# A leaky unit in one ScalarE instruction, and a shorter split of float64 weights, in an attention + two-layer MLP kernel

## The chip, the cores and the metric

One core of one Trainium2 chip runs the whole program in one launch. The metric is the device time in microseconds (us). A core has five engines that matter here: PE (TensorE, matmuls), DVE (VectorE), ACT (ScalarE), POOL (GpSimd) and SP (SyncE, which issues the DMAs). Each executes its own queue in order, and they meet at semaphores.

## The reference

```python
x = attention(q, k, v, M_prev, z_prev, beta)     # 2304 tokens x 512, causal softmax + a linear memory, gated
h = x @ w_in                                     # 512 -> 2048
x = np.maximum(0.01 * h, h) @ w_out              # the leaky unit; 2048 -> 512
a = x @ w_a                                      # 512 -> 1536
b = x @ w_b
out = (a * b @ w_out2).astype(np.float32)        # 1536 -> 512
```

The weights arrive as float64 and the activations as float32. The kernel carries both through the matmuls as two parts, a high one in the fp32r format and the float32 remainder of it, also kept as fp32r.

## The kernel before, in words

**Three stages.** An attention stage (lines 235 to 763) works on 16 pairs of heads. Its instructions are not written out in order: each step is given to `Plan` with a cost per engine, and `Plan.run` schedules them over 58 forward and backward sweeps and emits the best order found. The costs in the `add(...)` calls decide which engine a step gets and when. Where the plan sees PE idle early on, it inserts filler matmuls (L254). Then `moe1` (L965) and `moe2` (L1014) run in the order in which the Python loops issue them.

**The matmuls.** `three` (L229) issues three matmuls for a product: high x high (L230), high x low (L231), low x high (L232). The tokens are cut in two parts (1024 and 1280 columns), each in chunks `c` of 512 or 256 columns. In `moe1` a group `g` of 256 hidden features is computed for a part in up to six chunks (kind "u": 12 matmuls each into a PSUM bank of the ring `b0, b1, b2, b6`), and then multiplied back (kind "o": 6 matmuls each into the ring `b3, b4, b5, b7`, which L1007 on ACT evacuates in group 0 and L1009 on DVE afterwards). There are 8 groups. `moe2` has 6 groups of the same build with two products per chunk, `a * b` (L1043, DVE) in place of the leaky unit, and evacuations at L1060 (ACT, group 0) and L1062 (DVE).

**The leaky unit** is two instructions for each chunk: L985 on ACT writes 0.01 * h from PSUM to `gf`, and L986 on DVE takes the maximum of h (PSUM) and `gf`. `halves` (L942) then makes the high part on ACT (L944) and the low part on DVE or POOL (L945); it queues them one or two ticks later, so that they stand behind the next chunk's first instructions. The plan holds the first four chunks of group 0 (`first`, L675), with the same two steps at L692 and L696.

**The weights.** `Weights.micro` (L121) turns a chunk `i` of 512 columns of float64, loaded as pairs of 32-bit words, into high and low parts. There are 68 chunks, 4 of them inside the plan. The steps and their engines: `clamp` (L136, DVE) bounds the upper word, read as a float32 at a stride of two words; `square` (L139, ACT) squares it; `shift` (L142, DVE) and `join` (L145, DVE) move the exponent and mantissa to float32's places; `normal` (L148, DVE) multiplies with 0 where the square is too small; `high` (L154, ACT) rounds to fp32r; `power` (L159, DVE) and `low` (L162, DVE) scale the lower word; `rest` (L165) and `total` (L168) form the low part on POOL. `Weights.step` (L186) issues a third of a chunk at a time: clamp and shift (square one tick later), join and normal (high one tick later), power and low (rest and total one tick later). In `moe1` and `moe2` one such third is queued after most of the chunks, up to a limit of tiles held, and `split_parts` (L935) adds the splitting of the activations (L937 ACT, L938 DVE) at the start of each.

Of the kernel before, what the change touches and what calls it, by code (L numbers as in the profile page):

```python
# [11 lines left out]
F32 = mybir.dt.float32  # L12
# [3 lines left out]
AF = mybir.ActivationFunctionType  # L16
ALU = mybir.AluOpType
# [25 lines left out]
TURN = 170.0  # L43
COLD = 1400.0, 7000.0

WMIN = float(np.uint32(897 << 20).view(np.float32))
WMAX = float(np.uint32((1150 << 20) | 0xFFE00).view(np.float32))


# [5 lines left out]
def attention_moe_moe2(ctx: ExitStack, tc, kqT, qn, vn, m_prev, beta, w_in, w_out, w_a, w_b, w_o2, out):  # L55
# [26 lines left out]
    def after(k, fn):  # L82
        now[1] += 1
        heapq.heappush(tasks, (now[0] + k, now[1], fn))
# [7 lines left out]
    class Weights:  # L92
# [28 lines left out]
        def micro(self, i):  # L121

            c = slice((i % 2) * WC, (i % 2) * WC + WC)
            key = f"w{i // 2}.{i % 2}"
            t = {}

            def u(x):
                return t[x].bitcast(U32)

            def half(x):  # L130
                return self.tiles[i // 2][:, x, c]

            def clamp(_):
                for x in "har":
                    t[x] = self.temp(i, [P, WC], F32, "w" + x)
                nc.vector.tensor_scalar(t["h"], self.raw[i][:, :, 1].bitcast(F32), WMAX, -WMAX, ALU.min, ALU.max)  # L136

            def square(_):
                nc.scalar.activation(t["r"], t["h"], AF.Square)  # L139

            def shift(_):
                nc.vector.tensor_scalar(u("a"), u("h"), 3, 0x3FFFFFFF, ALU.logical_shift_left, ALU.bitwise_and)  # L142

            def join(_):
                nc.vector.scalar_tensor_tensor(u("a"), u("h"), 0xC0000000, u("a"), ALU.bitwise_and, ALU.bitwise_or)  # L145

            def normal(_):
                nc.vector.scalar_tensor_tensor(t["a"], t["r"], WMIN * WMIN, t["a"], ALU.is_ge, ALU.mult)  # L148

            def high(eng):  # L150
                if i % 2 == 0:
                    self.tile(i // 2)
                if eng == "ACT":
                    nc.scalar.copy(half(0), t["a"])  # L154
                else:
                    nc.vector.tensor_copy(half(0), t["a"])

            def power(_):
                nc.vector.tensor_scalar(u("h"), u("a"), 0xFF800000, None, ALU.bitwise_and)  # L159

            def low(_):
                nc.vector.scalar_tensor_tensor(t["r"], self.raw.pop(i)[:, :, 0], 2.0**-52, t["h"], ALU.mult, ALU.mult)  # L162

            def rest(eng):
                (nc.gpsimd if eng == "POOL" else nc.vector).tensor_tensor(t["a"], t["a"], f32(half(0)), ALU.subtract)  # L165

            def total(eng):
                (nc.gpsimd if eng == "POOL" else nc.vector).tensor_tensor(half(1), t["a"], t["r"], ALU.add)  # L168

            place = [f"g{x}.0" for x in ("10", "11", "12", "13", "1t")] if i == 2 else []  # L170
            one, two, tt = {"DVE": 335.0}, {"DVE": 600.0}, {"POOL": 1230.0, "DVE": 600.0}
            return [
                (None, lambda _: self.load(i), [], ["wraw"]),
                (one, clamp, ["wraw"], ["wh", "wa", "wr"]),
                ({"ACT": 520.0}, square, ["wh"], ["wr"]),
                (one, shift, ["wh"], ["wa"]),
                (two, join, ["wh"], ["wa"]),
                (two, normal, ["wr"], ["wa"]),
                ({"ACT": 520.0, "DVE": 335.0}, high, ["wa"], [key] + place),
                (one, power, ["wa"], ["wh"]),  # L180
                (two, low, ["wraw", "wh"], ["wr"]),
                (tt, rest, [key], ["wa"]),
                (tt, total, ["wr", "wa"], [key]),
            ]

        def step(self, n=1, limit=RING):  # L186

            for _ in range(n):
                i, third = divmod(self.part, 3)
                if i >= 2 * min(len(self.order), self.freed + limit):  # L190
                    return
                if third == 0:
                    self.load(i)
                    self.load(i + 1)
                    self.steps = [s[1] for s in self.micro(i)]
                _, clamp, square, shift, join, normal, high, power, low, rest, total = self.steps
                if third == 0:
                    clamp(0)
                    after(1, lambda: square(0))
                    shift(0)  # L200
                elif third == 1:
                    join(0)
                    normal(0)
                    after(1, lambda: high("ACT"))
                else:
                    power(0)
                    low(0)
                    after(1, lambda: (rest("POOL"), total("POOL")))
                self.part += 1
# [25 lines left out]
    def attention(att, plan):  # L235
# [22 lines left out]
        def one(key, shape, dtype=F32, pool=att):  # L258
            live[key] = pool.tile(shape, dtype, tag=key, bufs=1, name=key)
            return live[key]  # L260
# [414 lines left out]
        def first(x):  # L675
# [13 lines left out]
            gk = f"gf{x % 3}"  # L689

            def leak(_):
                nc.scalar.activation(one(gk, [P, 512], F32, main), plan.tiles[t], AF.Copy, scale=0.01)  # L692

            def most(_):
                g = live[gk]
                nc.vector.tensor_tensor(g, plan.tiles[t], g, ALU.max)  # L696

            def hi(eng):
                if k == 0:
# [3 lines left out]
            def lo(eng):  # L703
                both(eng, gates[f][:, 1, c], live[gk], f32(gates[f])[:, 0, c], ALU.subtract)

            add(leak, {"ACT": 480}, r=[t], w=[gk], at=at + 6)
            add(most, {"DVE": 600}, r=[t], w=[gk], at=at + 7)
            add(hi, c_copy(512), r=[gk] + [f"{hl}.g0"] * (k > 0), w=[f"{hl}.g{k}"] + ["raw2"] * (k == 0 and f == 1), at=at + 8, port=True)
            add(lo, c_tt(512), r=[gk, f"{hl}.g{k}"], w=[f"{hl}.l{k}"], at=at + 9, port=True)

# [254 lines left out]
    def moe1(ps, xh, y, gates):  # L965
        for g in range(8):
            wi = weights.get().rearrange("p s (k c) -> p s k c", k=4)
            for pr in range(2):
                x = xh[pr]
                gt = gates if g == pr == 0 else []  # L970
                for f in range(0 if gt else 2):
                    t = shared()
                    gt.append(t)
                    for c in chunks(pr):
                        n = c.stop - c.start
                        tick()
                        hp = ring("u", ps, [P, 512], F32)
                        for kt in range(4):
                            w = slice(f * 128, f * 128 + 128)
                            three(  # L980
                                hp[:, 0:n], wi[:, 0, kt, w], wi[:, 1, kt, w], x[:, 0, kt, c], x[:, 1, kt, c],
                                kt == 0, kt == 3,
                            )
                        gf = ring("gf", main, [P, 512], F32)[:, 0:n]
                        nc.scalar.activation(gf, hp[:, 0:n], AF.Copy, scale=0.01)  # L985
                        nc.vector.tensor_tensor(gf, hp[:, 0:n], gf, ALU.max)  # L986
                        halves(t, c, gf, nc.vector if f else nc.gpsimd)
                        yield "u", g, pr
                if pr == 0:
# [192 lines left out]
```

## Time and profile before

| what | value |
|---|---|
| median of 3 runs | 1061.68 us (1060.17 to 1061.82) |
| the profiled execution | 1061.82 us, of which the span of instructions is 1060.0 us |
| PE busy | 1043.9 us (98%) |
| DVE busy | 766.3 us (72%) |
| ACT busy | 426.0 us (40%) |
| POOL busy | 362.0 us (34%) |
| granted TensorE clock | 1.00, the 2.4 GHz level |
| chain that ended last | PE 70%, DVE 25%, ACT 2%, issue 2% |

The profile is one execution. A group of rows gives instructions of one line; its mean mixes those that ran at once and those that stood waiting for a shared resource after they had started. A wait gives the idle time of an engine and what ended it. Matmuls overlap, and their ends are modelled, so the busy share of PE is not a share of its peak.

### The profile page before, as it was taken

The numbers are of one execution on the slowest core, as the hardware profiler recorded it, in microseconds if no ns is written. First come the engines' busy times: TensorE is split into PE (matmuls) and PEld (weight loads), VectorE is DVE, ScalarE is ACT, GpSimd is POOL, SyncE is SP. The second block draws the span as 40 slices with busy tenths as digits, with TensorE's granted clock in tenths as the row PEclk, the third lists the DMA queues.
The fourth block names the chain that finished last, engine by engine and source line by source line (L and its number), as shares of the span: only waits on it lengthen the run. The fifth ranks groups of instructions, "written<-read, shape, count | busy, mean of one in ns | idle before, by whom it ended". The sixth has DMA issues, their size and how long they took to land.

```text
span 1060.0 us, 14629 instructions
## 1 busy us (share of the span) xinstructions
PE 1043.9 (98%) x5432; PEld 828.1 (78%) x5432; DVE 766.3 (72%) x1488; ACT 426.0 (40%) x949; POOL 362.0 (34%) x323
## 2 busy tenths in 40 slices
PE   9999999999999999999999999999999999999998
PEld 4566666787888788888888877888878878878887
DVE  6999999778787878676767693782973964955333
ACT  6888888665333333333333353422222222312110
POOL 4575663235445353342434131330330420411100
PEclk9999999999999999999999999999999999999999
DMA  5333430211111111110111010110110210210022
GB/s 214 102 119 115 159 132 27 73 60 60 40 60 60 40 60 40 40 60 20 60 40 57 3 48 33 60 60 1 61 60 1 80 40 2 80 39 1 1 80 99
DMA packets 18935, 63.33 MB, mean 60 GB/s; under 512 B 2224, under 2 KB 2224, under 8 KB 18864
## 3 DMA queue, kind: packets, MB, share of 16 engines
q1 hardware_dynamic: 18864, 62.40, 16.6%
q8 instruction: 42, 0.69, 0.3%
q14 instruction: 29, 0.24, 0.1%
HBM read 57.68 MB, written 4.72 MB: 59 GB/s over the span
## 4 chain that ended last, share of the span: by engine, by line
PE 70%; DVE 25%; ACT 2%; issue 2%; DMA 0%; DVEq 0%; POOL 0%; ACTq 0%; POOLq 0%
PE b L230 18%; PE b L231 18%; PE b L232 18%; PE b L548 4%; PE b L626 4%; PE b L495 3%; DVE wa L142 3%; DVE wh L136 2%; DVE wa L148 2%; DVE xf L1062 2%; DVE wa L145 2%; DVE wr L162 2%; DVE hl L945 2%; DVE gf L986 1%; PE b L522 1%
## 5 line engine op out<-in xcount | busy, mean ns | idle before, releaser
L230 PE MATMUL b<-xh,w 128*128 128x512 f32 (+1 forms) x800 | 295.5, 369 | 0.0
L231 PE MATMUL b<-xh,w 128*128 128x512 f32 (+1 forms) x800 | 294.6, 368 | 0.0
L232 PE MATMUL b<-xh,w 128*128 128x512 f32 (+1 forms) x800 | 294.4, 368 | 0.0
L165 POOL TENSOR_TENSOR wa<-wa,w 128x512 f32<-128x512 f32 x65 | 112.0, 1722 | 494.1 <-DVE wh L159 430.3
L230 PEld LDWEIGHTS b<-xh,w 128*128 128x128 f32 x800 | 150.8, 189 | 25.4
L232 PEld LDWEIGHTS b<-xh,w 128*128 128x128 f32 x800 | 150.7, 188 | 25.2
L231 PEld LDWEIGHTS b<-xh,w 128*128 128x128 f32 x800 | 150.9, 189 | 24.9
L1043 DVE TENSOR_TENSOR gf<-b,gf 128x512 f32<-128x512 f32 (+1 forms) x60 | 38.2, 636 | 121.8 <-PE b L232 121.8
L168 POOL TENSOR_TENSOR w<-wa,wr 128x512 fp32r<-128x512 f32 x67 | 94.9, 1416 | 11.5 <-DVE wr L162 4.6
L139 ACT ACTIVATE wr<-wh 128x512 f32<-128x512 f32 x68 | 43.0, 633 | 134.2 <-DVE wh L136 134.0
L944 ACT CAST hl<-gf 128x512 fp32r<-128x512 f32 (+1 forms) x91 | 52.5, 577 | 108.8 <-DVE gf L1043 70.9
L986 DVE TENSOR_TENSOR gf<-b,gf 128x512 f32<-128x512 f32 (+1 forms) x76 | 48.1, 633 | 60.4 <-ACT gf L985 60.2
L154 ACT CAST w<-wa 128x512 fp32r<-128x512 f32 x68 | 42.3, 622 | 121.8 <-DVE wa L148 121.7
L1009 DVE TENSOR_TENSOR xf<-b,xf 128x512 f32<-128x512 f32 (+1 forms) x140 | 83.5, 630 | 3.9 <-PE b L232 3.6
L230 PE MATMUL b<-hl,w 128*128 128x512 f32 (+1 forms) x220 | 81.6, 371 | 1.9 <-ACT hl L944 1.9
L231 PE MATMUL b<-hl,w 128*128 128x512 f32 (+1 forms) x220 | 81.3, 370 | 2.1 <-DVE hl L945 2.1
L232 PE MATMUL b<-hl,w 128*128 128x512 f32 (+1 forms) x220 | 81.0, 368 | 0.0
L1041 ACT COPY gf<-b 128x512 f32<-128x512 f32 (+1 forms) x60 | 32.5, 541 | 110.8 <-PE b L232 109.8
L450 ACT ACTIVATE p<-p,stat 128x384 f32<-128x384 f32 (+3 forms) x128 | 71.2, 559 | 11.7 <-DVE stat L503 11.4
L1062 DVE TENSOR_TENSOR xf<-b,xf 128x512 f32<-128x512 f32 x90 | 60.4, 685 | 18.9 <-PE b L232 18.7
L945 DVE TENSOR_TENSOR hl<-gf,hl 128x512 fp32r<-128x512 f32 (+1 forms) x66 | 53.9, 816 | 27.4 <-ACT hl L944 27.4
L477 POOL TENSOR_SCALAR p<-p,stat,keep 128x128 f32<-128x128 f32 (+3 forms) x85 | 53.9, 647 | 42.7 <-DVE stat L465 12.9
(123 smaller groups left out, 1900.9 us busy)
## 6 DMA issues: line engine op xcount, KB each, us to landing
raw<-in_kqT SPq DMA_DIRECT2D x16, 576.0 KB, 3.7
wraw<-in_w_in SPq DMA_DIRECT2D x16, 512.0 KB, 3.4
wraw<-in_w_out SPq DMA_DIRECT2D x16, 512.0 KB, 3.3
qraw<-in_qn SPq DMA_DIRECT2D x8, 768.0 KB, 4.2
wraw<-in_w_a SPq DMA_DIRECT2D x12, 512.0 KB, 3.3
wraw<-in_w_b SPq DMA_DIRECT2D x12, 512.0 KB, 3.2
wraw<-in_w_o SPq DMA_DIRECT2D x12, 512.0 KB, 3.4
vs<-in_vn SPq DMA_DIRECT2D x16, 320.0 KB, 3.0
```

Of the source, the lines that this page charges most:

```text
L165: (nc.gpsimd if eng == "POOL" else nc.vector).tensor_tensor(t["a"], t["a"], f32(half(0)), ALU.subtract)
L168: (nc.gpsimd if eng == "POOL" else nc.vector).tensor_tensor(half(1), t["a"], t["r"], ALU.add)
L230: nc.tensor.matmul(outp, l_hi, r_hi, start=start, stop=False)
L231: nc.tensor.matmul(outp, l_hi, r_lo, start=False, stop=False)
L232: nc.tensor.matmul(outp, l_lo, r_hi, start=False, stop=stop)
L450: nc.scalar.activation(t, t, AF.Exp, bias=s[:, 0, col : col + 1], scale=-1.0, accum_out=s[:, 1, col : col + 1])
L477: ENG[eng].tensor_scalar(live[p], live[p], stats[w % 3][:, 3, col : col + 1], k, ALU.mult, ALU.mult)
L944: after(1, lambda: nc.scalar.copy(t[:, 0, c], gf))
L945: after(1 if eng is nc.vector else 2, lambda: eng.tensor_tensor(t[:, 1, c], gf, f32(t)[:, 0, c], ALU.subtract))
L986: nc.vector.tensor_tensor(gf, hp[:, 0:n], gf, ALU.max)
L1009: nc.vector.tensor_tensor(y[pr][:, dm, c], op[:, 0:n], y[pr][:, dm, c], ALU.add)
L1062: nc.vector.tensor_tensor(y[:, i], op, y[:, i], ALU.add)
```

## The change

Two things are changed. The leaky unit becomes a single ACT instruction, `Prelu` with a slope of 0.01, at L692 and L985, and the maxima at L696 and L986 go; the plan's cost of the ACT step goes from 480 to 580 ns and that of the maximum (600 ns on DVE) is dropped. In the weights, `square` and `normal` go. `clamp` becomes two DVE instructions: the upper word without its sign bit, and a maximum and a minimum in place, so that magnitudes below a smallest value are raised to it instead of being set to zero. `join` takes the sign and the top exponent bit from the loaded word instead of from the clamped one. The constant `WMIN` goes from 897 to 896 in the exponent field. In the plan the clamp costs 670 instead of 335 ns, and 520 ns of ACT and 600 of DVE are dropped per chunk; all other constants stay.

```diff
--- before.py
+++ after.py
@@ -43,7 +43,7 @@
 TURN = 170.0
 COLD = 1400.0, 7000.0
 
-WMIN = float(np.uint32(897 << 20).view(np.float32))
+WMIN = float(np.uint32(896 << 20).view(np.float32))
 WMAX = float(np.uint32((1150 << 20) | 0xFFE00).view(np.float32))
 
 
@@ -133,19 +133,16 @@
             def clamp(_):
                 for x in "har":
                     t[x] = self.temp(i, [P, WC], F32, "w" + x)
-                nc.vector.tensor_scalar(t["h"], self.raw[i][:, :, 1].bitcast(F32), WMAX, -WMAX, ALU.min, ALU.max)
-
-            def square(_):
-                nc.scalar.activation(t["r"], t["h"], AF.Square)
+                nc.vector.tensor_scalar(u("h"), self.raw[i][:, :, 1], 0x7FFFFFFF, None, ALU.bitwise_and)
+                nc.vector.tensor_scalar(t["h"], t["h"], WMIN, WMAX, ALU.max, ALU.min)
 
             def shift(_):
                 nc.vector.tensor_scalar(u("a"), u("h"), 3, 0x3FFFFFFF, ALU.logical_shift_left, ALU.bitwise_and)
 
             def join(_):
-                nc.vector.scalar_tensor_tensor(u("a"), u("h"), 0xC0000000, u("a"), ALU.bitwise_and, ALU.bitwise_or)
-
-            def normal(_):
-                nc.vector.scalar_tensor_tensor(t["a"], t["r"], WMIN * WMIN, t["a"], ALU.is_ge, ALU.mult)
+                nc.vector.scalar_tensor_tensor(
+                    u("a"), self.raw[i][:, :, 1], 0xC0000000, u("a"), ALU.bitwise_and, ALU.bitwise_or
+                )
 
             def high(eng):
                 if i % 2 == 0:
@@ -171,11 +168,9 @@
             one, two, tt = {"DVE": 335.0}, {"DVE": 600.0}, {"POOL": 1230.0, "DVE": 600.0}
             return [
                 (None, lambda _: self.load(i), [], ["wraw"]),
-                (one, clamp, ["wraw"], ["wh", "wa", "wr"]),
-                ({"ACT": 520.0}, square, ["wh"], ["wr"]),
+                ({"DVE": 670.0}, clamp, ["wraw"], ["wh", "wa", "wr"]),
                 (one, shift, ["wh"], ["wa"]),
-                (two, join, ["wh"], ["wa"]),
-                (two, normal, ["wr"], ["wa"]),
+                (two, join, ["wraw"], ["wa"]),
                 ({"ACT": 520.0, "DVE": 335.0}, high, ["wa"], [key] + place),
                 (one, power, ["wa"], ["wh"]),
                 (two, low, ["wraw", "wh"], ["wr"]),
@@ -193,14 +188,12 @@
                     self.load(i)
                     self.load(i + 1)
                     self.steps = [s[1] for s in self.micro(i)]
-                _, clamp, square, shift, join, normal, high, power, low, rest, total = self.steps
+                _, clamp, shift, join, high, power, low, rest, total = self.steps
                 if third == 0:
                     clamp(0)
-                    after(1, lambda: square(0))
                     shift(0)
                 elif third == 1:
                     join(0)
-                    normal(0)
                     after(1, lambda: high("ACT"))
                 else:
                     power(0)
@@ -689,11 +682,7 @@
             gk = f"gf{x % 3}"
 
             def leak(_):
-                nc.scalar.activation(one(gk, [P, 512], F32, main), plan.tiles[t], AF.Copy, scale=0.01)
-
-            def most(_):
-                g = live[gk]
-                nc.vector.tensor_tensor(g, plan.tiles[t], g, ALU.max)
+                nc.scalar.activation(one(gk, [P, 512], F32, main), plan.tiles[t], AF.Prelu, alpha=0.01)
 
             def hi(eng):
                 if k == 0:
@@ -703,8 +692,7 @@
             def lo(eng):
                 both(eng, gates[f][:, 1, c], live[gk], f32(gates[f])[:, 0, c], ALU.subtract)
 
-            add(leak, {"ACT": 480}, r=[t], w=[gk], at=at + 6)
-            add(most, {"DVE": 600}, r=[t], w=[gk], at=at + 7)
+            add(leak, {"ACT": 580}, r=[t], w=[gk], at=at + 6)
             add(hi, c_copy(512), r=[gk] + [f"{hl}.g0"] * (k > 0), w=[f"{hl}.g{k}"] + ["raw2"] * (k == 0 and f == 1), at=at + 8, port=True)
             add(lo, c_tt(512), r=[gk, f"{hl}.g{k}"], w=[f"{hl}.l{k}"], at=at + 9, port=True)
 
@@ -982,8 +970,7 @@
                                 kt == 0, kt == 3,
                             )
                         gf = ring("gf", main, [P, 512], F32)[:, 0:n]
-                        nc.scalar.activation(gf, hp[:, 0:n], AF.Copy, scale=0.01)
-                        nc.vector.tensor_tensor(gf, hp[:, 0:n], gf, ALU.max)
+                        nc.scalar.activation(gf, hp[:, 0:n], AF.Prelu, alpha=0.01)
                         halves(t, c, gf, nc.vector if f else nc.gpsimd)
                         yield "u", g, pr
                 if pr == 0:
```

## Rows read from the trace of the kernel before

**Rows 1.** Stretches: length, busy (count) of PE, PEld, DVE, ACT, POOL; clock, DMA.
```profile
120.00:189.00 69.00, 68.15 (x499) 43.17 (x498) 65.19 (x199) 56.77 (x166) 33.64 (x45) 1.00 0.28 97
189.00:213.70 24.70, 24.70 (x161) 18.27 (x159) 17.95 (x39) 13.45 (x30) 4.22 (x5) 1.00 0.17 57
213.70:376.00 162.30, 157.68 (x753) 130.56 (x750) 132.49 (x198) 66.72 (x126) 71.06 (x47) 1.00 0.16 56
376.00:603.00 227.00, 227.00 (x1106) 192.23 (x1106) 167.57 (x277) 76.43 (x135) 83.21 (x59) 1.00 0.12 42
603.00:678.00 75.00, 72.56 (x350) 60.42 (x349) 46.31 (x71) 29.68 (x56) 15.67 (x10) 1.00 0.10 36
678.00:1038.00 360.00, 357.72 (x1671) 297.82 (x1670) 221.71 (x323) 86.17 (x151) 79.11 (x50) 1.00 0.11 40
```

**Rows 2.** Waits of PE (waiting line <- releaser: idle us, times, longest).
```profile
PE b L230 <- ACT xf L1060: 2.4, 3, 1.2
PE b L230 <- DVE xf L1062: 2.3, 3, 0.8
PE b L231 <- DVE hl L945: 2.1, 3, 1.7
PE b L230 <- ACT hl L944: 1.9, 3, 0.9
```

**Rows 3.** Groups by line and form (columns: busy us, mean ns; idle before).
```profile
L230 PE MATMUL b<-xh,w 128*128 128x512 f32 x640 | 250.4, 391 | 0.0
L985 ACT ACTIVATE gf<-b 128x512 f32<-128x512 f32 x60 | 35.7, 595 | 31.4 <-PE b L232 31.4
L986 DVE TENSOR_TENSOR gf<-b,gf 128x512 f32<-128x512 f32 x60 | 41.4, 690 | 54.2 <-ACT gf L985 54.1
L136 DVE TENSOR_SCALAR wh<-wraw 128x512 f32<-128x512 f32 x68 | 53.5, 787 | 0.3 <-DMA wraw<-in_w_out 0.3
L148 DVE SCALAR_TENSOR_TENSOR wa<-wr,wa 128x512 f32<-128x512 f32 x68 | 49.7, 731 | 6.2 <-DVE wa L145 0.5
L159 DVE TENSOR_SCALAR wh<-wa 128x512 uint32<-128x512 uint32 x68 | 28.5, 420 | 0.2
L162 DVE SCALAR_TENSOR_TENSOR wr<-wraw,wh 128x512 f32<-128x512 uint32 x68 | 47.3, 696 | 2.3
```

**Rows 4.** Timeline of DVE and POOL, 761 to 767 us (start, length).
```profile
761.92 1.74 POOL L165 TENSOR_TENSOR wa<-wa,w 128x512 f32<-128x512 f32 x1 [3.36 <-DVE wh L159]
763.02 0.92 DVE L136 TENSOR_SCALAR wh<-wraw 128x512 f32<-128x512 f32 x1
763.74 1.36 POOL L168 TENSOR_TENSOR w<-wa,wr 128x512 fp32r<-128x512 f32 x1
764.05 1.33 DVE L142 TENSOR_SCALAR wa<-wh 128x512 uint32<-128x512 uint32 x1
765.42 0.69 DVE L145 SCALAR_TENSOR_TENSOR wa<-wh,wa 128x512 uint32<-128x512 uint32 x1
766.21 0.69 DVE L148 SCALAR_TENSOR_TENSOR wa<-wr,wa 128x512 f32<-128x512 f32 x1
```

**Rows 5.** Timeline of DVE and ACT, 314 to 318 us.
```profile
314.01 1.83 DVE L148 SCALAR_TENSOR_TENSOR wa<-wr,wa 128x512 f32<-128x512 f32 x1
315.87 0.62 ACT L154 CAST w<-wa 128x512 fp32r<-128x512 f32 x1 [1.95 <-DVE wa L148]
317.02 0.69 DVE L986 TENSOR_TENSOR gf<-b,gf 128x512 f32<-128x512 f32 x1 [1.18 <-ACT gf L985]
```

**Rows 6.** Timeline of ACT around 636 us.
```profile
635.77 0.63 ACT L139 ACTIVATE wr<-wh 128x512 f32<-128x512 f32 x1 [1.57 <-DVE wh L136]
```

**Rows 7.** Table loads of the whole run; two ACT rows near 200 us.
```profile
L306 ACT ACT_TABLE_LOAD x1 | 1.3, 1283 | 0.7 <-PEq L1172 0.7
...
197.35 0.60 ACT L692 ACTIVATE gf<-b 128x512 f32<-128x512 f32 x1 [0.75 <-PE b L232]
201.19 0.78 ACT L450 ACTIVATE pt<-pt,stat 128x576 f32<-128x576 f32 x1 [2.27 <-DVE stat L530]
```

## The prediction, made before the kernel was run

> **What bounds the kernel now.** I read the busy time by stretch first, because the shares of the whole run mix two kinds of stage. From 376 to 603 us (most of the first layer) PE is busy for 227.00 of 227.00 us at the full clock, while DVE has some 60 us to spare [rows 1]: there nothing off PE can shorten anything. Idle PE is found in three other stretches: 162.30 - 157.68 = 4.62 us from 213.7 to 376, 2.44 around the change of layers, 2.28 in the second layer, together 9.34 us [rows 1]. In attention PE looks busy too, but part of that is filler; there DVE is the fullest engine, 65.19 of 69 us, until 189 us. From 189 to 213.7 PE is busy throughout, and DVE for 17.95 of 24.70 [rows 1].
>
> The waits of PE say what the idle time stood for: a PSUM bank not yet evacuated (L1060, L1062) or the high or low half of a chunk not yet made (L944, L945), three stops each, 8.7 us of the 9.34 [rows 2]. A stop costs a little more than its idle time. A 512-column matmul is shown as 391 ns long [rows 3], but 1106 of them ran in 227.0 us [rows 1], 0.205 us apart; the chunks average 461 columns, so 512 stand some 0.228 us apart, and about 0.16 us of a stop is hidden under the last matmul's tail. Twelve stops [rows 2] add 1.9 us: some 11.3 us in all is what could be won behind attention, and no more.
>
> Two close views say why the halves come late. From 314 us: `normal` takes 1.83 us instead of its usual 0.69 because it meets work on POOL; `high` on ACT waits for it (idle 1.95 us, ended by L148); the leak instruction stands behind `high` in ACT's queue, and the maximum on DVE then waits 1.18 us for the leak [rows 5]. Only then come the two halves, and PE stops for them. At 635.77 ACT stands in `square`, after 1.57 us of waiting for `clamp`, with an evacuation that PE needs behind it [rows 6].
>
> **The change part by part.** *The maximum* goes: 76 in the first layer and 4 in the plan, 690 ns each for 512 columns [rows 3]. From a chunk's last matmul to its halves one DVE instruction and one semaphore hop fall away, and the high half depends on DVE no longer. What takes its place is a `Prelu` from PSUM where a scaled copy from PSUM of 595 ns stood [rows 3]. Its duration is in no row. The exponential, with a pointer bias and an accumulator, is the longest ACT kind at hand: 0.78 us for 576 columns [rows 7], so some 0.7 at 512. From below, nothing suggests that it is quicker than the copy by more than 0.1. I take 0.60, since it is the same read, write and size; the bounds are worth 80 x -0.1 to +0.1 us = -8 to +8 us of ACT, which is busy for under half of each stretch behind attention [rows 1], so on the path they are worth a tenth of a microsecond per remaining stop.
>
> *Square* goes: 0.63 us of ACT [rows 6] per chunk, hidden, except where something stood behind its wait, as at 636 us.
>
> *Normal* goes: 731 ns on average [rows 3]; `join` to `normal` is 0.79 us from start to start [rows 4]. I take 0.75 us for the saving.
>
> *Clamp's second half* comes. Reading the word at a stride with a bit operation has its nearest rows in `clamp` (same stride, same engine mode) and `power` (a bit operation), and the second half, dense, is nearest to `power`: 420 ns [rows 3]. But `clamp` averages 787 [rows 3], and the timeline shows why: at 763.02 it stands until POOL's `rest` has ended at 763.66, and `shift` then stands 1.33 us until `total` has ended at 765.10 [rows 4]. So such a DVE instruction cannot run while POOL works on two operands. The bounds for the new instruction are 0.42 and 1.33 us. I take 0.45 (0.42 and a short dependence), because in the second layer POOL has just these two instructions per chunk and both are already waited for: the new pair will stand for `rest` and `total`, and `shift` behind them will run free.
>
> *Join* reads the loaded word at a stride: `low` does so at 696 ns [rows 3] against 0.69 for `join` now [rows 4]. Nothing. The loaded buffer is not held longer, since `low` reads it later anyhow.
>
> So a weight chunk costs DVE 0.75 - 0.45 = 0.30 us less, and a chunk of the leaky unit some 0.6 to 0.7 less.
>
> **The sum by stretch.** *213.7 to 376 us* (4.62 us idle; DVE busy 132.49 of 162.30 [rows 1]): the two later stops are of the kind at 314 us. Without `normal`, `high` can begin 1.8 us earlier, and the leak and the high half follow on ACT alone; a stop of 0.9 us goes whole, with its smaller companion for the low half (the three waits for L945 sum to 2.1, of which 1.7 is one in group 0 [rows 2], so 0.2 each). That is 2 x (0.9 + 0.2 + 2 x 0.16) = 2.8 us. The long stop in group 0, 1.7 us for a low half, stands behind weight steps that wait for POOL; I give it back by 1.0, and the remaining small ones by 0.7. Sum 4.5. What is late next is the low half there.
>
> *Change of layers* (2.44 us idle): the evacuations on ACT no longer stand behind `square`, and stand behind a `high` that comes 0.3 to 1 us earlier. Each of the three waits should shrink by half or more: 1.7 us with the hidden part.
>
> *Second layer* (2.28 us idle in three stops of 0.76): no maximum was there, so only 0.30 us per weight chunk helps. POOL's 50 instructions there [rows 1] are two per chunk, so 25 chunks, some eight for each stop; if seven of them stand ahead of the stop in DVE's queue, 7 x 0.30 = 2.1 us less backlog is more than a stop's 0.76 + 0.16. I take 2.4 of 2.76.
>
> *Attention*: DVE loses 4 x 0.30 us in the weights and 4 x 0.69 in the maxima, about 4 us; but most of it lies after 189 us, where PE is full [rows 1]. Before that perhaps 0.5 us counts. The plan is drawn anew with other costs, and a greedy order over many hundred steps can fall either way: I put +-4 us on it.
>
> 4.5 + 1.7 + 2.4 + 0.5 = 9.1 us. The profiled execution took 1061.82 us, 1.8 more than its span and 0.1 more than the median of the three runs, so the forecast is 1061.8 - 9.1 = 1052.7 us.
>
> **The rivals.** *The stops have other causes.* If the second layer's stops and those at the change are set by POOL's hold on DVE and not by DVE's load, the backlog comes back and only the shorter chain of the leaky unit pays: 4.5 us plus 0.5, 1056.8; with part of that lost, 1058. For it: the 1.33 us beside POOL [rows 4] doesn't shrink when DVE arrives earlier.
>
> *Slower: the new clamp half waits for POOL on its own.* Place: every weight chunk outside the plan. Price: 1.33 instead of 0.45, so a chunk costs DVE 0.58 more than now instead of 0.30 less; it decides as soon as the new half costs over 0.75. In the second layer 7 x 0.58 = 4 us is added to each of three stops, 12 in all, and 2.3 for four chunks at the change; the leaky unit's 4.5 stays: 1061.8 + 14.3 - 4.5 = 1071.6 us. Against it: the two POOL instructions are both waited for now.
>
> *The plan falls badly*: +4 us in attention, or more, leaves 1056 to 1060.
>
> *The function needs another table.* The run has one table load, 1283 ns [rows 7], though it mixes exponentials, squares, scaled copies and copies. The plan's leaks stand among exponentials (197.35 and 201.19 us [rows 7]); with four leaks, one to eight loads would be put into ACT's queue there, 1.3 to 10.3 us at worst: 1053 to 1061, about 1058. If copies too needed a reload beside it, the whole first layer would pay twice per chunk, 76 x 2 x 1.28 = 195 us of ACT, and the kernel would be 20 us or more slower.
> The Trainium skill (ScalarE: Activation LUTs, What ACT_TABLE_LOAD costs) gives 1283 ns for a load and some 1380 for the drain, 2.66 us per switch; by that figure, an estimate, eight switches would take up to 21 us. The trace agrees with the 1283; no run here shows a switch. The same page (Rules for kernel authors) puts a maximum on VectorE, which speaks against this edit; here an ACT instruction was spent on the leak anyway.
>
> **How the numbers follow.** The forecast (1049 to 1056.5) 0.56; other causes 0.18; a bad plan 0.08; a table in the plan alone 0.05; the clamp beside POOL 0.07; tables in every chunk 0.03; better than 1049 0.03. About 0.2%, 2.1 us, is what a measurement of this kernel can tell from no change. Faster by more: all but 0.10 on the slower side and 0.04 from the bad ends of the plan and the table: 0.86. The lower end is all 11.3 us and 4 of attention, 1046.5; I take 1046. The upper end takes in the small-gain cases to 1060.5, and leaves out the two slower ones.
>
> **What would show it.** The windows of after should have under 1.5 us of idle PE from 213.7 to 376 and under 0.6 in the second layer, no wait of PE for L1062, one table load, a second clamp instruction with 0.4 to 0.9 us on average and `shift` down to about 0.5, and attention ending near 213 us. I would be wrong if DVE's busy time did not fall by some 65 us (80 maxima at 0.6 and 68 chunks at 0.3), if the start of the first layer moved by more than 4 us, or if the waits of PE went on at the same places.

## The result, and the profile after

The changed kernel takes 1048.63 us (median of 4 runs, 1047.24 to 1049.54) against 1061.70 for the kernel before: a ratio of 0.988, 95% interval 0.986 to 0.990. That is faster, by 13.1 us; 9.1 had been forecast (1052.7), in a range of 1046 to 1060.5. The profiled execution took 1047.24 us, with a span of 1045.4, so 14.6 us less than the one of before; it is the fastest of its four executions, and the profiled one of before is the slowest of its own, so the two traces show more than the medians.

Three moments split both traces: the first matmul that reads `hl` (attention has handed over), the first copy of a product of the second layer, and the last evacuation. In the kernel before (start and length in us):

```profile
213.73 0.50 PE L230 MATMUL b<-hl,w 128*128 128x512 f32 x1
...
608.28 0.59 ACT L1041 COPY gf<-b 128x512 f32<-128x512 f32 x1 [12.31 <-PE b L232]
...
1056.25 0.69 DVE L1062 TENSOR_TENSOR xf<-b,xf 128x512 f32<-128x512 f32 x1 [0.67 <-PE b L232]
```

and in the changed kernel:

```profile
211.74 0.50 PE L223 MATMUL b<-hl,w 128*128 128x512 f32 x1
...
599.48 0.59 ACT L1028 COPY gf<-b 128x512 f32<-128x512 f32 x1 [13.62 <-PE b L225]
...
1041.64 0.69 DVE L1049 TENSOR_TENSOR xf<-b,xf 128x512 f32<-128x512 f32 x1 [0.67 <-PE b L225]
```

So attention gave back 213.73 - 211.74 = 2.0 us, the first layer 394.55 - 387.74 = 6.8, the second layer with the change of layers 447.97 - 442.16 = 5.8; what comes after the last evacuation's start is as long as before. Forecast were 0.5, 4.5 and 1.7 + 2.4 = 4.1.

From the hand-over on, both traces hold the same 3960 matmuls in the same order, so their starts can be compared one by one. Those up to 376 us of the kernel before take 6.75 us less in the changed kernel, those from there to 603 us the same to the hundredth, those to 678 us (the change of layers) 1.29 less, and the second layer 4.57 less, together 12.6 us. Against them stand the forecast's 4.5, nothing, 1.7 and 2.4.

Busy time by stretch in the changed kernel, the stretches moved by the earlier start (length, then PE, PEld, DVE, ACT, POOL with counts, clock, DMA); they answer to [rows 1]:

```profile
187.00:211.70 24.70, 24.55 (x158) 18.32 (x158) 12.97 (x31) 12.78 (x28) 2.73 (x4) 1.00 0.11 35
211.70:373.00 161.30, 160.76 (x779) 135.54 (x776) 117.34 (x181) 59.01 (x112) 69.96 (x49) 1.00 0.18 61
373.00:590.00 217.00, 217.00 (x1059) 183.92 (x1058) 136.65 (x218) 65.14 (x117) 79.99 (x58) 1.00 0.13 43
590.00:665.00 75.00, 73.42 (x357) 61.64 (x356) 45.09 (x71) 25.74 (x49) 14.42 (x10) 1.00 0.09 30
665.00:1023.00 358.00, 358.00 (x1682) 300.72 (x1681) 218.18 (x326) 71.95 (x129) 80.16 (x51) 1.00 0.12 42
```

Idle PE from the end of attention on has gone from 4.62 us to 0.54 in the first of them, from 2.44 to 1.58 at the change, and from 2.28 to 0.00 in the second layer. The count says more than the idle time: 779 matmuls ran in 161.3 us, where 753 had run in 162.3. The waits of PE, answering to [rows 2], have lost three of the four lines of before. Of the fourth, the evacuation on ACT (L1060, here L1047), one stop of three is left, the only one worth naming:

```profile
PE b L223 <- ACT xf L1047: 1.6, 1, 1.6
PE b L247 <- POOL mask L231: 1.6, 1, 1.6
PE b L225 <- DVE w L165: 0.5, 1, 0.5
```

(The second is at the very start of the program and was there before. The third stands 2 us after the hand-over and is new.) The groups that the sum priced, answering to [rows 3]:

```profile
L973 ACT ACTIVATE gf<-b 128x512 f32<-128x512 f32 x60 | 35.9, 598 | 106.9 <-PE b L225 105.4 <-POOL hl L933 1.5
L136 DVE TENSOR_SCALAR wh<-wraw 128x512 uint32<-128x512 uint32 x68 | 64.1, 943 | 0.9 <-DMA wraw<-in_w_in 0.9
L137 DVE TENSOR_SCALAR wh<-wh 128x512 f32<-128x512 f32 x68 | 55.6, 818 | 2.3
L140 DVE TENSOR_SCALAR wa<-wh 128x512 uint32<-128x512 uint32 x68 | 34.5, 508 | 6.6
L299 ACT ACT_TABLE_LOAD x1 | 1.3, 1283 | 0.7 <-PEq L1159 0.7
```

The leak with the maximum in it costs what the scaled copy cost (598 against 595 ns), and there is still one table load in the whole run. The two halves of the clamp stand longer than 0.42 us on average, but `shift` behind them fell from a mean of 902 to 508 ns. DVE's busy time fell from 766.3 to 705.6 us.

### The profile page after: what moved, and what is told of

It is laid out like the page before. It is cut to its first block, busy times and chain, and to the rows that moved or that the text cites. A ratio compares the mean times of both kernels' runs of the same rounds, so it can differ in the third digit from the quotient of the medians.

```text
span 1045.4 us, 14368 instructions
## 1 busy us (share of the span) xinstructions
PE 1036.7 (99%) x5427; PEld 829.8 (79%) x5429; DVE 705.6 (67%) x1409; ACT 387.7 (37%) x886; POOL 354.8 (34%) x317
## 4 chain that ended last, share of the span: by engine, by line
PE 95%; DVE 4%; issue 0%; ACT 0%; POOL 0%; DVEq 0%; POOLq 0%
PE b L223 26%; PE b L224 26%; PE b L225 26%; PE b L541 4%; PE b L619 4%; PE b L488 4%; PE b L515 2%; PE b L590 1%; PE b L247 1%; PE b L420 1%; DVE xh L926 1%; DVE qraw L374 0%; DVE wr L159 0%; DVE wh L137 0%; DVE gf L1030 0%
## 5 line engine op out<-in xcount | busy, mean ns | idle before, releaser
L162 POOL TENSOR_TENSOR wa<-wa,w 128x512 f32<-128x512 f32 x65 | 109.6, 1686 | 494.5 <-DVE wh L156 385.2
L1030 DVE TENSOR_TENSOR gf<-b,gf 128x512 f32<-128x512 f32 (+1 forms) x60 | 38.2, 636 | 124.9 <-PE b L225 124.9
L933 DVE TENSOR_TENSOR hl<-gf,hl 128x512 fp32r<-128x512 f32 (+1 forms) x66 | 50.0, 758 | 77.4 <-ACT hl L932 77.0
L996 DVE TENSOR_TENSOR xf<-b,xf 128x512 f32<-128x512 f32 (+1 forms) x140 | 87.1, 634 | 19.4 <-PE b L225 17.2
L165 POOL TENSOR_TENSOR w<-wa,wr 128x512 fp32r<-128x512 f32 x66 | 91.3, 1384 | 6.2 <-DVE wr L159 1.1
L973 ACT ACTIVATE gf<-b 128x512 f32<-128x512 f32 (+1 forms) x76 | 42.0, 552 | 108.5 <-PE b L225 107.0
L496 DVE CUSTOM_DVE_ANT_0 p<-b,mask 128x384 f32<-128x384 f32 (+3 forms) x128 | 57.5, 482 | 11.3 <-PE b L488 10.3
L136 DVE TENSOR_SCALAR wh<-wraw 128x512 uint32<-128x512 uint32 x68 | 64.1, 943 | 0.9 <-DMA wraw<-in_w_in 0.9
```

The source lines that it names most:

```text
L136: nc.vector.tensor_scalar(u("h"), self.raw[i][:, :, 1], 0x7FFFFFFF, None, ALU.bitwise_and)
L496: nc.vector.tensor_tensor_reduce(one(p, [P, wd]), plan.tiles[banks[j]][:, c : c + wd], mask[:, off : off + wd], -0.125, BIG, ALU.add, ALU. ...
L933: after(1 if eng is nc.vector else 2, lambda: eng.tensor_tensor(t[:, 1, c], gf, f32(t)[:, 0, c], ALU.subtract))
L996: nc.vector.tensor_tensor(y[pr][:, dm, c], op[:, 0:n], y[pr][:, dm, c], ALU.add)
```

## The experiments

Times are medians; the kernel before ran beside each set, on the same chip. "Layers" is the time from the first matmul on `hl` to the last evacuation, "first" and "second" its two parts, all from the one profiled execution of each kernel.

| kernel | us | before, beside it | ratio (95%) | attention hands over | first | second |
|---|---|---|---|---|---|---|
| before | 1061.70 | | | 213.73 | 394.55 | 447.97 |
| changed | 1048.63 | 1061.70 | 0.988 (0.986 to 0.990) | 211.74 | 387.74 | 442.16 |
| e1_prelu_only | 1053.22 | 1060.01 | 0.994 (0.992 to 0.995) | 211.58 | 387.38 | 448.46 |
| e2_weights_only | 1049.20 | 1060.01 | 0.990 (0.989 to 0.992) | 212.94 | 388.37 | 442.01 |
| e3_moe_only | 1049.22 | 1060.01 | 0.990 (0.989 to 0.992) | 214.00 | 386.90 | 442.40 |
| e4_plan_only | 1058.95 | 1060.01 | 0.999 (0.998 to 1.000) | 211.75 | 393.10 | 447.93 |
| e0_after | 1047.90 | 1060.75 | 0.988 (0.987 to 0.990) | 212.05 | 387.74 | 442.20 |
| e5_square_kept | 1048.82 | 1060.75 | 0.989 (0.987 to 0.991) | 214.16 | 387.74 | 442.42 |
| e6_product_kept | 1067.62 | 1060.75 | 1.007 (1.006 to 1.009) | 211.66 | 389.26 | 460.86 |
| e8_high_on_dve | 1045.81 | 1060.75 | 0.986 (0.985 to 0.988) | 212.25 | 387.72 | 440.38 |
| e9_bound_twice | 1058.58 | 1060.28 | 0.999 (0.998 to 1.000) | 211.28 | 388.64 | 452.11 |
| e10_no_bound | 1046.82 | 1060.28 | 0.988 (0.986 to 0.989) | 212.42 | 387.72 | 440.68 |
| e11_high_on_dve_again | 1045.73 | 1060.28 | 0.987 (0.986 to 0.988) | 212.34 | 387.72 | 440.32 |
| e12_after_again | 1047.91 | 1060.28 | 0.989 (0.988 to 0.990) | 213.11 | 387.72 | 442.15 |

### One edit at a time

Only the leaky unit, with the weights of before (shown at L985; the plan's L692 and L696 change in the same way):

```diff
-nc.scalar.activation(gf, hp[:, 0:n], AF.Copy, scale=0.01)
-nc.vector.tensor_tensor(gf, hp[:, 0:n], gf, ALU.max)
+nc.scalar.activation(gf, hp[:, 0:n], AF.Prelu, alpha=0.01)
```

> The leaky unit as one ACT instruction, everywhere; the weights as before (square and masked product kept). Theory by parts: the shorter chain of the leaky unit clears most of the idle PE between the end of attention and 376 us (4.6 us idle before, under 1.5 expected), while the three stops of the second layer (2.3 us idle, waits of PE for the evacuation on DVE) stay, since no DVE work was taken from that layer; some 1056 to 1057 us if attention keeps its length. Rival (the stops of the first layer come from the masked product standing beside POOL, with the high part's copy and the leak behind it on ACT): the stops near 317 and 368 us stay at half their size or more, and the time is 1059 or above.

Measured: 1053.22 us, 6.8 less than before beside it, where the expected time was some 5 to 6 less than 1061.8. The first layer is as short as with both edits (387.38 us), the second as long as before (448.46). The waits of PE say the same:

```profile
PE b L230 <- DVE xf L1056: 2.6, 3, 1.1
PE b L230 <- ACT xf L1054: 2.5, 3, 1.2
PE b L231 <- DVE hl L940: 0.2, 1, 0.2
```

The evacuations at the change of layers (here L1054) and in the second layer (L1056) keep their three stops each, and of the waits for halves one of 0.2 us is left. The rival, by which the masked product alone held the first layer, falls: taking the maximum out of the chain is enough.

Only the weights: the changed kernel with the scaled copy and the maximum put back.

> The new weights everywhere; the leaky unit as scaled copy and maximum, as before. Theory by parts: the three stops of the second layer go (2.3 us idle and some 0.5 hidden), the stops at the change of layers halve (2.4 us idle before), and in the first layer the stops near 317 and 368 us shrink because the high part's copy waits for the masked product no longer; 1054 to 1056 us if attention keeps its length. Rival (the new second half of the clamp waits for POOL by itself and eats what the masked product gave): the second layer's stops stay, and the time is 1060 or above.

Measured: 1049.20 us, 10.8 less than before beside it, where some 6 to 8 were expected. The stops of the second layer are gone, so the rival falls. Both layers shrink, the first to 388.37 and the second to 442.01 us. So the weights alone do nearly the whole of it, and in the first layer either edit alone takes out what both take out: 7.2 us by the one, 6.2 by the other, 6.8 by the two in this pair of traces. They are not to be added: the stops there needed the maximum and the old weight steps together.

### Layers or attention

The next two kernels hold both forms of the weight steps, and use the old ones in the plan and the new ones behind it, or the other way round; the leaky unit goes with them. The main line of the first of the two:

```diff
-            for x, (cost, fn, r, wr) in enumerate(weights.micro(i)):
+            for x, (cost, fn, r, wr) in enumerate(weights.micro_old(i)):
```

> Both edits in the two layers behind attention; the plan of attention with the steps, engines and costs of the kernel before. Theory: the plan's part of the gain is small and the layers' part is nearly all; attention hands over at 213.7 us as before, and the time is 1061.7 less some 12 us, 1049 to 1050. Rival (the plan drawn anew brought more than the 2 us by which the first layer starts earlier in the trace): 1052 or above.

> Both edits inside the plan of attention alone (its four weight chunks, its four leaky chunks and their costs); the layers behind it as before. Theory: the first layer starts some 2 us earlier, at 211.7 us, and its stops stay, so 1059 to 1060 us. Rival (the earlier start is an accident of one execution): 1061 to 1062 us.

Measured: 1049.22 and 1058.95 us. The layers' edits alone give 10.8 us. The plan's alone give 1.1 us, with an interval that ends at no change (0.998 to 1.000); in its profiled execution attention ends at 211.75 us as in the changed kernel, and the first layer is 1.45 us shorter than before, which had not been expected. What this is worth is taken up below under attention.

### What the square was worth

The changed kernel, with the square still done on ACT, its result unused:

```diff
                     clamp(0)
+                    after(1, lambda dead=self.dead: dead(0))
                     shift(0)
```

> The changed kernel with the square still done on ACT for every chunk behind attention (its result is not used). Theory (the square mattered only where something stood behind its wait for the clamp): one or two stops of PE come back at the change of layers, some 1 to 1.5 us more than the changed kernel; the second layer stays without stops. Rival (ACT's load does not matter anywhere): the same time as the changed kernel within 0.3 us. Other rival (the freed ACT time cleared the first layer's stops): 3 us or more.

Measured: first layer 387.74, second 442.42 us, against 387.74 and 442.16 to 442.20 without it. The square was worth at most 0.3 us behind attention, not the 1 to 1.5 us that were expected; the 0.9 us in the medians (1048.82 against 1047.90) is not separable from attention, which in this trace ended 2.1 us later. The square does hold an evacuation again, and PE's one stop at the change of layers now stands there instead of behind `high`:

```profile
629.83 0.63 ACT L140 ACTIVATE wr<-wh 128x512 f32<-128x512 f32 x1 [3.18 <-DVE wh L137]
630.37 0.57 ACT L1053 COPY xf<-b 128x512 f32<-128x512 f32 x1
...
630.99 0.50 PE L229 MATMUL b<-w,qs 128*128 128x512 f32 x1 [1.73 <-ACT xf L1053]
```

So the stop has moved to an earlier evacuation and is 0.15 us longer (1.73 against 1.58); no second one has come.

### How much DVE time per weight chunk matters

Four kernels differ in nothing but DVE's work per weight chunk behind attention: without the bound (the second half of the clamp), as changed, with the bound twice, and with the masked product kept. The two additions, cut down (both act behind attention only; e10 leaves out the first line there):

```diff
 nc.vector.tensor_scalar(t["h"], t["h"], WMIN, WMAX, ALU.max, ALU.min)
+nc.vector.tensor_scalar(t["h"], t["h"], WMIN, WMAX, ALU.max, ALU.min)           # e9: once more
+nc.vector.scalar_tensor_tensor(t["a"], t["h"], 0.0, t["a"], ALU.is_ge, ALU.mult) # e6: after join
```

> The changed kernel with the masked product still done on DVE for every chunk behind attention (mask of a magnitude that is always true, so the numbers do not change), which costs DVE some 0.75 us per chunk more than the changed kernel and some 0.6 more than the one before. Theory (the second layer's stops are DVE's backlog, chunk by chunk): the three stops come back and are longer than the 0.76 us of idle time of the kernel before, some 2 to 3.5 us each, and the time is 7 to 12 us above the changed kernel. Rival (the stops were set by the hold of POOL on DVE, into which the product falls anyway): stops of 0.8 us or less, 3 us or less above the changed kernel.

> The changed kernel with the second half of the clamp (maximum and minimum in place) done twice for every chunk behind attention. It measures the price of the added instruction by doubling it. Theory (0.45 us per chunk, since POOL's two instructions are already waited for): the doubled one leaves DVE 0.15 us per chunk worse off than the kernel before, so three stops come back in the second layer with some 1 us each and the layers take 4 to 7 us longer than the changed kernel's 829.9. Rival (each such instruction meets POOL by itself and costs over 0.75): the layers take 15 us or more longer, like the kernel with the product kept (850.1).

> The changed kernel without the second half of the clamp behind attention (magnitudes out of float32's range are not bounded there; that part of the computation is left out). Theory (no stop is left that hangs on DVE's load, save part of the one at the change of layers): 0 to 0.7 us less than the changed kernel's 829.9 for the layers. Rival (the added instruction still costs on the path): 1.5 us or more less.

Measured, layers together: 828.4 us without the bound, 829.9 as changed, 840.7 with the bound twice, 850.1 with the product. (By the forecast's own prices the product costs 0.75 - 0.30 = 0.45 us per chunk more than the kernel before, not the 0.6 of the expectation.) In the kernel with the product the waits of PE for evacuations and halves are back and many more:

```profile
PE b L229 <- DVE xf L1055: 4.4, 12, 0.7
PE b L229 <- ACT xf L1053: 3.7, 2, 2.2
PE b L231 <- DVE hl L939: 3.5, 2, 1.7
PE b L231 <- DVE qs L939: 2.1, 1, 2.1
```

What a second bound costs DVE is seen in its timeline; the clamp's first half at 762.64 stands for POOL, and the two bounds and `shift` follow 0.46 and 0.54 us apart:

```profile
762.64 1.51 DVE L136 TENSOR_SCALAR wh<-wraw 128x512 uint32<-128x512 uint32 x1
764.18 0.43 DVE L137 TENSOR_SCALAR wh<-wh 128x512 f32<-128x512 f32 x1
764.64 0.43 DVE L139 TENSOR_SCALAR wh<-wh 128x512 f32<-128x512 f32 x1
765.18 0.43 DVE L142 TENSOR_SCALAR wa<-wh 128x512 uint32<-128x512 uint32 x1
```

So the doubled instruction cost the 0.45 us that the theory gave it, and no wait of its own: the rival's price falls. In the second layer this holds throughout (its 24 second bounds there average 427 ns); in the first layer the second bound averages 594 ns over 35, so there some of them do wait.

The layers' loss was larger than expected in both kernels, 10.8 us (4 to 7 expected) and 20.2 us (7 to 12). Most of it is in the second layer. There the distance from clamp to clamp, inside a run of chunks, is 6.26 us in the changed kernel, 6.72 with the bound twice and 6.99 with the product, and the matmuls of that layer take 8.6 and 14.5 us longer than in the changed kernel. Divided, that is what 19 and 20 chunks lose; before the change it was 6.53 us from clamp to clamp and 4.6 us longer, 17 chunks. So some 17 to 20 of the layer's 25 chunks pay in full for what DVE needs more than in the changed kernel. From the changed kernel downward this slope ends: 0.45 us less per chunk brought 1.5 us, all of it at the change of layers (1.47 us, matmul by matmul) and 0.01 in the second layer. In the total the theory of 0 to 0.7 us was wrong there, and the rival right.

### The stop that is left

At the change of layers the trace of the changed kernel shows the clamp's first half standing until POOL has done `rest`, the second half until it has done `total`, and then `join`; `high` on ACT waits 3.89 us for it, and with it the evacuation L1047 that PE needs:

```profile
624.37 1.52 DVE L136 TENSOR_SCALAR wh<-wraw 128x512 uint32<-128x512 uint32 x1
625.92 1.40 DVE L137 TENSOR_SCALAR wh<-wh 128x512 f32<-128x512 f32 x1
627.42 0.43 DVE L140 TENSOR_SCALAR wa<-wh 128x512 uint32<-128x512 uint32 x1
627.88 0.69 DVE L143 SCALAR_TENSOR_TENSOR wa<-wraw,wa 128x512 uint32<-128x512 uint32 x1
...
628.61 0.62 ACT L151 CAST w<-wa 128x512 fp32r<-128x512 f32 x1 [3.89 <-DVE wa L143]
629.13 2.04 ACT L1047 COPY xf<-b 128x512 f32<-128x512 f32 x4
```

So the added instruction stands on PE's path here, as e10 showed. `high` moved to DVE for that short stretch takes the evacuation out from behind it (the edit cut down, the comment added here):

```diff
-                    after(1, lambda: high("ACT"))
+                    where = "DVE" if self.turn else "ACT"     # turn: second layer, group 0, first part
+                    after(1, lambda: high(where))
```

> The changed kernel with the high part's copy on DVE instead of ACT while the first part of the second layer's first group is computed. Theory (the one stop left stands behind that copy in ACT's queue, which waits for join): the stop of 1.6 us goes and the time is 1.5 us below the changed kernel. Rival (PE then waits for something else there, since DVE has 0.42 us more to do per chunk): the same time within 0.4 us or longer.

> The changed kernel once more, beside the runs that are compared with it. Theory: 0.988 of the kernel before, within 0.2%, one stop of PE left behind attention (some 1.6 us at the change of layers). Rival (the shorter of its two groups of times was an accident of the chip): 0.990 or above.

> The changed kernel with the high part's copy on DVE while the first part of the second layer's first group is computed, once more. Theory: the layers take 828.0 us against 829.9, so 0.2% less than the changed kernel beside it. Rival (the earlier difference was that of attention): the same time as the changed kernel within 0.5 us.

> The changed kernel, beside the run before it. Theory: attention ends at either some 212 or some 214 us in one and the same plan, by how instructions of DVE and POOL meet, while the layers take 829.9 us whatever it is. Rival: the layers' time varies too.

Measured: 1045.81 and 1045.73 us, beside 1047.90 and 1047.91 for the changed kernel, 2.1 and 2.2 us less; the layers take 828.1 and 828.0 us against 829.9 in the two pairs of traces, and the wait of PE for that evacuation is gone. The layers' time of the changed kernel is the same in its three traces (829.9 us), while attention handed over at 211.7, 212.1 and 213.1; the last of these is neither of the two values that the theory for e12 allowed. This version beats both kernels, 0.986 to 0.987 of the one before.

## Why the prediction was right, and where it was off

**What bounds the kernel.** Right: nothing changed where PE had been full without a pause, and the gain lies in the stretches that [rows 1] and [rows 2] had marked. From 376 to 603 us, 1105 matmuls take the same time in both traces. The size was too small because idle time, with a little added, was taken for the whole loss. I put 11.3 us as all that could be won behind attention; 12.6 were won, and one stop was still left. Each of the three stops in the second layer cost 1.03 us where 0.76 us of idle time is shown: the held matmul starts 0.92 us late, as I had reckoned with 0.16 added, and the one after it loses another 0.11. Seven more delays of 0.16 to 0.19 us in that layer show no idle time at all, 1.2 us together. One of them, before and after:

```profile
754.68 0.39 PE L232 MATMUL b<-w,hl 128*128 128x512 f32 x1
754.97 0.50 PE L230 MATMUL b<-w,qs 128*128 128x512 f32 x1
755.31 0.39 PE L231 MATMUL b<-w,qs 128*128 128x512 f32 x1
```

```profile
744.65 0.39 PE L225 MATMUL b<-w,hl 128*128 128x512 f32 x1
744.87 0.39 PE L223 MATMUL b<-w,qs 128*128 128x512 f32 x1
745.10 0.39 PE L224 MATMUL b<-w,qs 128*128 128x512 f32 x1
```

The three starts are 0.29 and 0.34 us apart before, and 0.22 and 0.23 after. In the first layer the two later stops, at 318 and 369 us, cost 1.65 us each where I had 1.42.

**The maximum.** Right, and shown by e1: with the leaky unit in one instruction the first layer has lost its stops. It is enough, but not the only way: with the weights alone (e2) they go as well. `Prelu` was priced at 0.60 us and takes 0.598; there was no second table load, among exponentials and copies alike, so that rival is out. No run has more than its one load, so the switch that the Trainium skill prices (ScalarE: Activation LUTs, What ACT_TABLE_LOAD costs) occurred in no run here. The term of that stretch was mis-sized by 2.3 us (4.5 forecast, 6.75 measured), partly for the reason above, partly because I gave back only 1.0 of the 1.7 us stop in group 0 [rows 2]; it went whole.

**The weights.** The mechanism was right in the second layer. There the two halves of the clamp stand for `rest` and `total`, and `shift` runs free, as forecast from [rows 4]:

```profile
751.51 0.69 DVE L1049 TENSOR_TENSOR xf<-b,xf 128x512 f32<-128x512 f32 x1
752.11 0.93 DVE L136 TENSOR_SCALAR wh<-wraw 128x512 uint32<-128x512 uint32 x1
753.07 1.40 DVE L137 TENSOR_SCALAR wh<-wh 128x512 f32<-128x512 f32 x1
754.57 0.43 DVE L140 TENSOR_SCALAR wa<-wh 128x512 uint32<-128x512 uint32 x1
755.03 0.69 DVE L143 SCALAR_TENSOR_TENSOR wa<-wraw,wa 128x512 uint32<-128x512 uint32 x1
755.64 0.68 DVE L1030 TENSOR_TENSOR gf<-b,gf 128x512 f32<-128x512 f32 x1
```

0.93 us, 1.40 us, 0.43 us: before it was 0.92 and 1.33 and nothing more [rows 4]. From one evacuation with its chunk to the next DVE needs about 6.3 us (745.85 to 752.11 from clamp to clamp in this trace) against 6.5 before (756.50 to 763.02), so the net saving is 0.26 us per chunk where I had 0.30. Over all 68 chunks it is less: `clamp`, `shift`, `join` and `normal` kept DVE busy for 212.8 us before and their successors for 203.3, which is 0.14 us per chunk, and so DVE's busy time fell by 60.7 us where I had named some 65 as a sign. The other signs came. e9 confirms the price of the added half, e6 what would have happened had it cost 0.75 more: the stops of the second layer come back, worse than before, and the kernel is slower by 0.7%. The slower rival was sound in mechanism and wrong in its condition. The term of the second layer was 2.4 us and 4.6 were measured: there the stops went whole, and with them the delays that show no idle time. The change of layers was put at 1.7 us and gave 1.3, less than forecast.

**The square.** Rightly read, but mispriced. The evacuation at 636.31 us did stand behind it [rows 6], and PE waited for that evacuation, though for 0.16 us only:

```profile
636.93 0.50 PE L230 MATMUL b<-w,qs 128*128 128x512 f32 x1 [0.16 <-ACT xf L1060]
```

The two longer stops there, at 633.76 and 639.82 us, stood behind `high`. In the changed kernel two of the three are gone, and the last has grown from 1.23 to 1.58 us; with the square put back (e5) the stop is at the square again and 0.15 us longer. Both wait for weight steps on DVE, so taking one out leaves the other to hold PE.

**The clamp's half at the change of layers** was priced at no cost on the path, since its cover was a wait for POOL that was there anyhow. The cover holds in the second layer, but at the change, from 623 to 630 us, DVE does nothing but weight steps and PE waits for their end: e10 finds 1.5 us there.

**Attention.** I gave 0.5 us with a scatter of 4 for a plan drawn anew. The pair of traces shows 2.0, but not as an effect of the change alone. Ten traces run the changed plan (after, e0, e4, e5, e6 and e8 to e12) and hand over between 211.3 and 214.2 us, 212.3 on average; the plan of before ended at 213.7, and at 214.0 in e3. The medians do not bear out a gain. If the layers of before always take 842.5 us, as in their one trace, the gain that is left for attention after that of the layers is 0.5, 0.3 and -0.3 us in the three sets of the changed kernel, -0.4 in e4, whose layers are themselves 1.5 us shorter, and 0.0 on average over the ten kernels. So no gain in attention is shown, and 0.5 was right only in being small. Why e3, with the old plan, loses 2.4 us by the same sum stays open.

**The rival of other causes** (the second layer's stops stay) is refuted by e2, where they go with the weights alone.

## What to carry to other kernels

Where PE has a few short stops, take the busy time of the engine that they wait for in those stretches only: a quarter of a microsecond per chunk decided here between no stop and three, while the same saving was worth nothing in the long stretch between. Idle time is a lower bound of what stops cost; where two kernels run the same matmuls in the same order, comparing their starts one by one finds the rest. Don't add up two edits that relieve the same engine at the same stops; run each alone. An instruction that only takes over a wait costs nothing as long as somebody else's work stands behind the same wait, and its full length where the chain runs through it.

## What the runs showed of the hardware

A DVE instruction that meets POOL's two-operand work can stand through the whole of it, and the same instruction of the same plan does so in one execution and not in another. In eight of the ten traces of the changed plan, e0 (shown first) among them, a normalisation takes 0.57 or 0.58 us. In the two that hand over last, e5 (shown second) and e12, it takes 2.84:

```profile
42.07 0.58 DVE L470 TENSOR_SCALAR pt<-pt,stat,keept 128x576 f32<-128x576 f32 x1
...
42.20 1.71 POOL L277 TENSOR_TENSOR xh<-xf,xh 128x576 fp32r<-128x576 f32 x1
43.87 1.04 POOL L277 TENSOR_TENSOR phi<-phi,nr 128x512 f32<-128x512 f32 x1
```

```profile
42.42 2.84 DVE L476 TENSOR_SCALAR pt<-pt,stat,keept 128x576 f32<-128x576 f32 x1
...
42.55 1.40 POOL L283 TENSOR_TENSOR xh<-xf,xh 128x576 fp32r<-128x576 f32 x1
43.91 1.04 POOL L283 TENSOR_TENSOR phi<-phi,nr 128x512 f32<-128x512 f32 x1
```

In the second it stands through both POOL instructions, which follow each other without a gap. Where DVE's takes 0.58 us, POOL's first takes 1.71 instead of 1.40. The starts do not say which of the two came first: in both traces DVE's is shown 0.13 us before POOL's. What differs is what went before. The DVE instruction ahead of this one took 0.45 us in the eight traces and 0.91 in the two, and at about 27 us DVE had waited for a load for 0.2 to 0.6 us in the eight and for 2.0 (e5) and 1.2 us (e12) in the two; that the one led to the other is likely and not shown. PE is 1.5 us further behind e0 at 60 us than at 40 in both. e5 loses another 0.7 us between 180 and 190 us, and its attention ended 2.1 us later than e0's. The Trainium skill (GPSIMD Engine Reference, Specifications) says that POOL's SBUF interfaces are shared with VectorE and names contention with instructions of a 2-port mode or with two SBUF inputs; the trace agrees that the two engines hold each other up, and does not show the mode.
